# Four small matmul tiles with the complex sum left to the accumulator, in a four-layer FFT kernel on one core

## The chip, the core and the metric

The kernel runs on 1 core of one Trainium2 chip. The metric is the device time of one execution in microseconds. The kernel before has a median of 785.24 us over 3 runs (784.71 to 789.31). One further execution was profiled: it took 786.58 us, and its trace spans 784.8 us, so 1.8 us lie outside the trace. TensorE is called PE (its weight loads PEld), VectorE DVE, ScalarE ACT, GpSimd POOL, SyncE SP.

## The reference

Four residual layers on x (2048 rows, 512 channels), A, B, A, B, each behind a layer norm. All is float32. The weights of both A layers, and of both B layers, are the same.

```python
def _A_ref(x, w_r, w_i):
    X = rfft2(x, axes=(-2, -1)) * (w_r + 1j * w_i)
    return irfft2(X, s=(S, D), axes=(-2, -1))

def _B_ref(u, log_A_real, A_imag, C_real, C_imag, log_dt, D_skip):
    ...
    P = exp((A * dt[:, None])[:, :, None] * pos)       # 512 channels x 128 states x 2048 steps
    K = 2.0 * einsum("dn,dnl->dl", C, P).real
    Kf, Uf = rfft(K, 2 * L), rfft(u_t, 2 * L)          # along time
    return irfft(Uf * Kf, 2 * L)[:, :, :L] + u * D_skip

x = x + _A_ref(layernorm(x), A_w_r, A_w_i)
x = x + _B_ref(layernorm(x), ...)
x = x + _A_ref(layernorm(x), A_w_r, A_w_i)
x = x + _B_ref(layernorm(x), ...)
```

What the change touches is B: a long convolution along time, done as a Fourier transform, a product of complex spectra and a transform back.

## The kernel before

**Stages.** The first A layer fills 0 to about 230 us. From about 120 to 454 us `kernel_time` builds the filter K in 64 half units; on the way its work is spread between that of other stages (the list `FILL`). `kernel_freq` transforms K (four blocks of 128 channels, called K blocks here) and `layer_b` runs the first B layer over four channel blocks b0 to b3, up to about 540 us. Then come the second A layer (to about 668 us) and the second B layer (to the end). In the first B layer the chain of blocks is b0, K1, b1, K2, b2, K3, b3; `kernel_time` steps lie between those of the first part.

**A block of the convolution.** For each block of 128 channels the following steps run; `blk` is the block, and each small matmul goes through the helper `side_by_side`, so that in the profile all of them have line L319 and must be told apart by their tiles.

- `rows` of `forward_b`: the first transform, 64 matmuls of 64x64 weights (a piece of the data, tile `w` or `x`) with 128 columns of the table `t`; then two ACT copies (L651) per four rows into a tile `z`.
- `turn`: eight 32x32-wise transposes on DVE (L657), `z` to `z`.
- `pair`: the second transform, in four pairs i. For each pair and each of two planes (real, imaginary: `pl`) two matmuls with 128x64 weights (table `mb`, half of which is zero, since two groups of 32 channels share it) write one PSUM tile of 128x512.
- `weigh`: the complex product. Per pair, DVE makes the four real products `wb` (L963: two planes of the signal by two planes `kk` of the filter) and a small correction (L965). Four additions or subtractions of 64x512 (L975) then join them into the tile `Y` (`u`): the list `YB` gives 12 of a block's 16 to POOL and 4 to DVE, and `YC`, for the last block of the second layer, 9 and 7.
- `units` of `back`: the first transform back, 8 units of 16 matmuls with weights from `Y`, 128x64, and 64 columns of `mb`; a 32-column matmul (L983) ahead of units 0 and 4; an ACT copy (L988) per unit into `V`. Units 0 to 3 (j=0) need pairs 0 and 1 alone, units 4 to 7 need pairs 2 and 3.
- `rows` of `back`: the second transform back, four times 8 matmuls with 128x64 weights and 128 columns, a DVE addition of 128x512 to the residual (L1002), in the first layer the layer norm's sums (L1007).

In a K block `keep` stands for `weigh`: ACT copies the spectrum into `kk` (L926), from where the first B layer takes it, and SP stores it to DRAM. DVE sets aside the entry at frequency 0 (L934 to L936). The second layer loads the spectra again (`kk<-kf`).

**Order.** `layer_b` writes the order of steps by hand, with those of the block before and the block after between the four pairs of a block:

```python
steps = [[now[0], *turns, *last[:2]], [now[1], *last[2:4], *then[1][:1], *last[4:6]],
         [now[2], *last[6:], *then[1][1:2], *units[:2]], [now[3], *units[2:4], *then[1][2:], *then[2][:4]]]
turns, last = then[2][4:], [*units[4:], *rows]
```

(`now`: pairs with `weigh`; `last`: the rest of the block before; `then[1]`, `then[2]`: `rows` and `turn` of the next block.) A scheduler moves instructions on each engine from there by its own estimate. Buffers are given out in turn: `p1`, `p2` and `p3` are PSUM tiles, with 5 banks for p1 and p3 together and 3 for p2 in the B layers (`PB`). `u` has two buffers (Y and V), `wb` eight, `kk` eight, `kw` (the rounded phases of `kernel_time`) two, `qp` five.

## Time and profile before

| | |
|---|---|
| median of 3 runs | 785.24 us |
| the profiled execution | 786.58 us |
| span of its trace | 784.8 us |
| busy, share of the span: PE, DVE | 612.4 us (78%), 646.6 us (82%) |
| ACT, POOL | 420.4 us (54%), 415.4 us (53%) |
| mean granted TensorE clock | 0.90 |
| DMA | 80.26 MB, mean 102 GB/s |

Busy time is the time in which at least one instruction of an engine was running; several small matmuls that run side by side count once. The `mean ns` of a group is that of one instruction. A float32 matmul of the code stands as two instructions in the trace: the 1024 matmuls of `units` in both layers are 2048 rows. Shares over the whole span mix stages with different limits, so the stages are read one by one.

### The profile page before, as it was taken

What the parts mean: (1) busy time and instruction counts of PE and PEld (TensorE: products, weight loads), DVE (VectorE), ACT (ScalarE), POOL (GpSimd) and SP (SyncE); (2) the same over time, 40 slices, a digit from 0 to 9 for tenths busy, and PEclk for the clock granted to TensorE, in tenths of its full rate; (3) what the DMA queues carried; (4) which work ended last, traced back from release to release, by engine and by line L of the source; (5) the groups of instructions that cost most, each with busy time, mean ns of one, the idle gap of its engine ahead of it and who ended that gap; (6) DMA issues with size and microseconds to landing.
All of it is one profiled execution on the core that took longest, in us unless ns stands there. A gap on an engine that the chain in (4) does not pass through costs nothing. (4 is left out here: it accounts for less than half of the span.)

```text
span 784.8 us, 20886 instructions
## 1 busy us (share of the span) xinstructions
PE 612.4 (78%) x8208; PEld 417.6 (53%) x8208; DVE 646.6 (82%) x1301; ACT 420.4 (54%) x919; POOL 415.4 (53%) x596
## 2 busy tenths in 40 slices
PE   3337788698758687897867977865899897889986
PEld 2336566464424342654343645644877664466666
DVE  7999749889997769968996977878587598789993
ACT  3434788755556676787477833323766335243322
POOL 3675886766625226732675166281055473375850
PEclk9656999998975999899989999997999898799998
DMA  8300651343547232452326359422122004134403
GB/s 320 117 0 1 147 124 49 102 101 129 125 161 148 72 105 49 129 139 79 43 67 146 113 120 252 133 82 81 54 82 83 28 14 147 56 91 128 145 24 105
DMA packets 144257, 80.26 MB, mean 102 GB/s; under 512 B 78656, under 2 KB 123840, under 8 KB 143264
## 3 DMA queue, kind: packets, MB, share of 16 engines
q1 hardware_dynamic: 143904, 78.51, 36.0%
q8 instruction: 65, 1.06, 0.5%
q0 software_dynamic: 256, 0.43, 0.3%
q14 instruction: 32, 0.26, 0.1%
HBM read 54.30 MB, written 25.03 MB: 101 GB/s over the span
## 5 line engine op out<-in xcount | busy, mean ns | idle before, releaser
L975 POOL TENSOR_TENSOR u<-wb,wb 64x512 f32<-64x512 f32 x90 | 137.0, 1523 | 81.2 <-DVE wb L963 74.5
L319 PE MATMUL p<-z,mb 128*64 128x512 f32 (+1 forms) x480 | 104.0, 543 | 13.2 <-DVE wb L963 5.8
L651 ACT COPY z<-p 128x512 f32<-128x512 f32 x96 | 51.5, 595 | 70.5 <-PE p L319 47.0
L861 DVE TENSOR_TENSOR qp<-qp,mag 128x1024 f32<-128x1024 f32 x64 | 83.3, 1305 | 1.2
L963 DVE TENSOR_TENSOR wb<-p,kk 128x512 f32<-128x512 f32 x128 | 80.6, 674 | 4.0 <-PE p L319 4.0
L859 DVE SCALAR_TENSOR_TENSOR qp<-qp,mag 128x256 f32<-128x256 f32 x128 | 63.6, 512 | 18.7 <-ACT qp L805 18.4
L319 PEld LDWEIGHTS p<-mb,u 128*64 128x64 f32 x2048 | 67.6, 146 | 17.9 <-issue 9.6
L319 PE MATMUL p<-mb,u 128*64 128x64 f32 x2048 | 69.9, 231 | 8.6 <-DVE u L975 4.2
L657 DVE STREAM_TRANSPOSE z<-z 128x512 f32<-128x512 f32 x96 | 58.5, 673 | 21.1 <-ACT z L651 21.1
L1087 POOL TENSOR_SCALAR w<-w,norms 128x128 f32<-128x128 f32 x64 | 37.8, 604 | 62.7 <-DMA w<-h 59.7
L530 DVE TENSOR_TENSOR w<-wt,p 128x514 f32<-128x514 f32 x64 | 42.5, 687 | 32.4 <-PE p L319 24.2
L535 POOL TENSOR_TENSOR w<-w,w 64x257 f32<-64x257 f32 x48 | 40.0, 834 | 53.7 <-DVE w L530 45.8
L872 PEld LDWEIGHTS pv<-qp 128*32 128x32 f32 x2048 | 38.0, 120 | 53.8 <-issue 20.2
L805 ACT ACTIVATE kf<-pk 128x512 f32<-128x512 f32 x64 | 38.8, 606 | 48.7 <-PE pk L841 48.4
L459 PE MATMUL p<-w,w 128*128 128x128 f32 x128 | 32.1, 429 | 40.6 <-DVE w L452 30.9
L319 PEld LDWEIGHTS p<-z,mb 128*64 128x64 f32 x480 | 34.4, 142 | 50.5 <-issue 30.9
L319 PE MATMUL p<-t,w 64*64 64x128 f32 x1024 | 48.1, 309 | 16.7 <-DMA w<-kt 8.1
L872 PE MATMUL pv<-qp 128*32 128x64 f32 x2048 | 51.6, 240 | 8.2 <-DVE qp L861 5.3
L988 ACT COPY u<-p 128x512 f32<-128x512 f32 x64 | 37.4, 589 | 38.1 <-PE p L319 38.1
L840 DVE TENSOR_SCALAR kw<-pk 128x512 bf16<-128x512 f32 x64 | 43.0, 679 | 13.3 <-PE pk L839 13.3
L319 PEld LDWEIGHTS p<-t,w 64*64 64x64 f32 x1024 | 36.8, 152 | 29.0 <-DMA w<-kt 10.7
L459 PEld LDWEIGHTS p<-w,w 128*128 128x128 f32 x128 | 27.8, 318 | 44.6 <-issue 24.7
(198 smaller groups left out, 1498.1 us busy)
## 6 DMA issues: line engine op xcount, KB each, us to landing
wt<-in_w SPq DMA_DIRECT2D x32, 257.0 KB
kf<-kk SPq DMA_DIRECT2D x32, 256.0 KB
kk<-kf SPq DMA_DIRECT2D x32, 256.0 KB
u<-in_x SPq DMA_DIRECT2D x16, 256.0 KB
hr<-in_x SPq DMA_DIRECT2D x16, 256.0 KB
kt<-stage SPq DMA_DIRECT2D x32, 128.0 KB
h<-hr SPq DMA_DIRECT2D x16, 256.0 KB
w<-kt SPq DMA_DIRECT2D x32, 128.0 KB
```

The costliest lines, as they stand in the source:

```text
L319: last = self.nc.tensor.matmul(out, weights, data, start=not more, stop=True, skip_group_check=True).ins
L459: nc.tensor.matmul(p[:, b], xf[:, b], t, start=True, stop=True)
L530: nc.vector.tensor_mul(m[pl], W, px[:, None, :].to_broadcast([128, 2, 257]))
L535: e[0].tensor_sub(Y[0:64, v], m[0][hs, 0], m[1][hs, 1])
L651: nc.scalar.copy(tiles["z"][:, :, :, b, m:m + 2].rearrange("p u j m r -> p (u j) (m r)"), ps[b].rearrange("p u j m r -> p (u j) (m r)"))
L657: nc.vector.transpose(tiles["zt"][:, u:u + 8].rearrange("p u j d -> p (u j d)"), tiles["z"][:, u:u + 8].rearrange("p u j b m r -> p (u j b ...
L840: nc.vector.tensor_scalar(whole, p, MAGIC, -MAGIC, op0=ALU.add, op1=ALU.add)
L859: nc.vector.scalar_tensor_tensor(QP[:, c, 0], QP[:, c, 1, :, ::-1], -1.0 if c else 1.0, m[:, 0], op0=ALU.mult, op1=ALU.mult)
L861: nc.vector.tensor_mul(t, t, mag[:, None, 1:3, 256 * j:256 * j + 256].to_broadcast([128, 2, 2, 256]))
L872: nc.tensor.matmul(p[32 * t:32 * t + 32, g], QP[:, c, 2, d], QP[:, c, 0:2, d], start=c == 0, stop=c == 1, tile_position=(0, 32 * t), skip_ ...
L963: nc.vector.tensor_mul(split(m[c, pl], "du", [32, 16]), by_channel(p), split(k[c], "du", [32, 16]))
L975: self.added = e[0].tensor_sub(y[0:64], v[0, 0], v[1, 1]), e[1].tensor_add(y[64:128], v[0, 1], v[1, 0])
```

## The change

**Quarter tiles.** `rows` of `forward_b` now uses weights of 64x32 (twice as many matmuls, eight positions instead of four). `pair` uses 64x64 weights: the contraction is over 64 rows, so the zeros of the old table are gone, and a PSUM tile of 128x512 is made by two matmuls in each of two tiles q at once. `pair` takes a list of tables `kinds`.

**The complex sum in PSUM.** In the first layer `pair` uses the table `DUP`, which makes the real and the imaginary plane of the signal's spectrum in two copies of its rows ("signal products doubled"); DVE multiplies each by the filter's spectrum as it lies in `kk`. In the second layer `pair` uses the plain table `NAT`, and each plane of the filter is loaded from DRAM with its rows doubled ("second K loaded doubled"). Either way there are 16 products of 128x512 per block as before, but they go to two tiles M[0] and M[1], and no addition joins them. `units` multiplies M[0] and M[1] by two tables and lets PSUM add: 64 matmuls of 64x64 per unit of eight channels, 4 units per block. `rows` of `back` does likewise with 64x64 weights, and adds to the residual in halves of 256 columns (L1035 of the new kernel). A step `mix` of four 32-column matmuls replaces the two L983.

**Order and buffers.** Every unit contracts over all four pairs, so units come after `now[3]`, with the next block's `turn` between them. `u` has three buffers (M[0], M[1], V). The buffers of `wb` and `xw` are gone, `w` serves the residual too and has six buffers instead of seven, `kw` one instead of two, `qp` four instead of five, and `kernel_time` ends a half unit three steps after it begins it instead of four (`LAGV`). PSUM has 4 and 4 banks in the B layers (`PB`). The spectra are stored from ACT's queue, and the output from POOL's for the first three blocks (`DQ`). The second A layer's `even` lies in `kk`.

The core of the diff:

```diff
-DQ = ''
+DQ = 'UaOg'
-PB = [5, 3]
+PB = [4, 4]
-LAGV = 4
+LAGV = 3
-QP = 5
+QP = 4
...
-        def pair(i, use):
-            last = None
-            for pl in range(2):
-                p = self.ps("p2", [512])
-                products = []
-                for h in (1, 0):
...
-                    products += [(o[:, 0], MB[:, 0, pl], z[:, 0])] * c + [(o[:, c:], MB[:, 1, pl], z[:, u + c:u + 16])]
-                last = self.side_by_side(products, last)
-                use(pl, p)
+        def pair(i, use, kinds):
+            z = tiles["zt"]
+            last = None
+            for x, K in enumerate(kinds):
+                ps = [self.ps("p2", [512]) for q in range(2)]
+                products = []
+                for first in (1, 0) if i == 0 else (0,):
+                    us = slice(16 * i, 16 * i + 1) if first else slice(16 * i + (i == 0), 16 * i + 16)
+                    for j in range(2):
+                        for q in range(2):
...
+                            products.append((o, K[64 * q:64 * q + 64, 1 - first], z[64 * q:64 * q + 64, us, j]))
+                last = self.side_by_side(products, last)
+                for q in range(2):
+                    use(x, q, ps[q])
...
-            def use(pl, p):
-                for c in range(2):
-                    m[c, pl] = self.sb("wb", [512])
-                    nc.vector.tensor_mul(split(m[c, pl], "du", [32, 16]), by_channel(p), split(k[c], "du", [32, 16]))
...
-                self.added = e[0].tensor_sub(y[0:64], v[0, 0], v[1, 1]), e[1].tensor_add(y[64:128], v[0, 1], v[1, 0])
+            own = kept is not None
...
+                        part = bass.AP(tensor=part.tensor, offset=part.offset, ap=[part.ap[0], [0, 2], part.ap[1]])
+                        self.dma("W")(k[x][q], part)
+                        if i == 0:
+                            nc.gpsimd.tensor_copy(split(k[x][q], "du", [32, 16])[:, :, 0], self.kf0[:, blk, q, x])
+            def use(x, q, p):
+                for o in (x,) if own else range(2):
+                    nc.vector.tensor_mul(M[o][:, q, :, 16 * i:16 * i + 16], by_channel(p),
+                                         split(k[q] if own else k[o][q], "du", [32, 16]))
+            pairs[i](use, self.DUP if own else self.NAT)
...
-                p = self.ps("p3", [64, 8])
-                self.side_by_side([(p[64 * r:64 * r + 64, :, i], Y[:, j, d + i], MBT[:, 64 * r:64 * r + 64])
-                                   for i in range(8) for r in range(2)])
+                ps = [self.ps("p3", [64, 8]) for j in range(2)]
+                self.side_by_side([(ps[j][64 * q:64 * q + 64, :, i], m[64 * j:64 * j + 64, q, d + i],
+                                    self.MT[64 * j:64 * j + 64, x], *[True] * x)
+                                   for i in range(8) for x, m in enumerate(M) for j in range(2) for q in range(2)])
...
+            steps = [now[0], *last[:1], *special, now[1], *last[1:], now[2], *then[1][:2], now[3], *then[1][2:]]
+            turns = then[2]
+            for n in range(4):
+                steps += [*units[n:n + 1], *turns[2 * n:2 * n + 2]]
+            last = rows
```

Three places show what moves. In the second B layer, DVE at the start of the last block has this order before (L963 a product, L965 the correction, L975 an addition of two products into Y, which is `u`):

```order
L963 TENSOR_TENSOR wb_8560<-p_1709_8556,kk_8552 128x512
L963 TENSOR_TENSOR wb_8562<-p_1709_8556,kk_8553 128x512
L963 TENSOR_TENSOR wb_8568<-p_1712_8564,kk_8552 128x512
L965 TENSOR_TENSOR wb_8568<-p_1712_8564,kf_1_65 64x32
L963 TENSOR_TENSOR wb_8571<-p_1712_8564,kk_8553 128x512
L963 TENSOR_TENSOR wb_8627<-p_1720_8624,kk_8620 128x512
L963 TENSOR_TENSOR wb_8629<-p_1720_8624,kk_8621 128x512
L975 TENSOR_TENSOR u_7827<-wb_8560,wb_8571 64x32x16
```

and now this (L993 a product, into one of the two M tiles; L1035 the residual of the block before):

```order
L993 TENSOR_TENSOR u_9289<-p_1734_11386,kk_11378 128x32x16
L993 TENSOR_TENSOR u_9290<-p_1734_11386,kk_11380 128x32x16
L993 TENSOR_TENSOR u_9289<-p_1735_11387,kk_11379 128x32x16
L993 TENSOR_TENSOR u_9290<-p_1735_11387,kk_11381 128x32x16
L1035 TENSOR_TENSOR za_6500<-za_6500,p_1727_11299 128x4x2x32 x2
L1035 TENSOR_TENSOR za_6500<-za_6500,p_1728_11300 128x4x2x32 x2
L993 TENSOR_TENSOR u_9289<-p_1742_11476,kk_11468 128x32x16
```

The additions of products are gone, and the residual's additions stand between the products. On PE, where a block of the second layer gives way to the next, the last four units stand directly ahead of the next block's first pair before:

```order
L319 MATMUL p_1690_8413<-mb_2788,u_7827 64x64 x16
L319 MATMUL p_1691_8431<-mb_2788,u_7827 64x64 x16
L319 MATMUL p_1700_8471<-mb_2788,u_7827 64x64 x16
L319 MATMUL p_1701_8489<-mb_2788,u_7827 64x64 x16
L319 MATMUL p_1709_8556<-z_8547,mb_2788 64x512
```

Now all 256 matmuls of the block's units (64 to a unit) stand behind the next block's `rows`; this is where they begin, four positions in turn, first M[0], then M[1] onto the same columns:

```order
L330 MATMUL p_1617_9643<-t_8859,x_8863 32x64x2
L330 MATMUL p_1618_9678<-mb_2805,u_9289 64x64 x2
L330 MATMUL p_1619_9679<-mb_2805,u_9289 64x64 x2
L330 MATMUL p_1618_9678<-mb_2805,u_9290 64x64 x2
L330 MATMUL p_1619_9679<-mb_2805,u_9290 64x64 x2
```

On DVE at the end of `kernel_time` (L861 before, L888 now, is its last multiplication), the sums of b1 and the transposes of b2 follow it before, ahead of b2's products:

```order
L861 TENSOR_TENSOR qp_5203<-qp_5203,mag_4831 128x2x512
L1007 BN_STATS stats_66<-xw_5465 128x6 x4
L1007 BN_STATS stats_66<-xw_5500 128x6 x4
L657 STREAM_TRANSPOSE z_5598<-z_5378 128x512 x8
L963 TENSOR_TENSOR wb_5644<-p_1116_5640,kk_5234 128x512
```

Now b2's products follow it at once, since those sums and transposes have moved in front of it:

```order
L888 TENSOR_TENSOR qp_5886<-qp_5886,mag_5437 128x2x512
L886 SCALAR_TENSOR_TENSOR qp_5987<-qp_5987,mag_5437 128x256 x2
L888 TENSOR_TENSOR qp_5987<-qp_5987,mag_5437 128x2x512
L993 TENSOR_TENSOR u_3391<-p_1104_6503,kk_6014 128x32x16
L993 TENSOR_TENSOR u_3391<-p_1105_6504,kk_6015 128x32x16
```

More of the change, by code (lines that the diff above doesn't have):

```diff
@@ L1025, in layer_b @@
                     f()
-            now, units, rows = pairs, [], []
+            now, units, rows, special = pairs, [], [], []
             if blk is not None:
-                now = [partial(weigh, blk, pairs, i, *[YC] * (not more and blk == 3)) for i in range(4)]
+                now = [partial(weigh, blk, pairs, i) for i in range(4)]
                 units, rows = back(blk)
+                special = [mix]
             then = chain[i + 1] if i + 1 < len(chain) else (None, [], [])
@@ L1034, in layer_b @@
                 then = chain[-1]
-            steps = [[now[0], *turns, *last[:2]], [now[1], *last[2:4], *then[1][:1], *last[4:6]],
-                     [now[2], *last[6:], *then[1][1:2], *units[:2]], [now[3], *units[2:4], *then[1][2:], *then[2][:4]]]
-            turns, last = then[2][4:], [*units[4:], *rows]
-            steps = sum(steps, [])
+            steps = [now[0], *last[:1], *special, now[1], *last[1:], now[2], *then[1][:2], now[3], *then[1][2:]]
[3 more added lines that the diff above has]
+            last = rows
             half = len(steps) // 2
@@ L1155, in net_kernel @@
             at = cuts[1]
-            wide, folds, banks = ExitStack(), ExitStack(), ExitStack()
+            wide, folds, banks, second = ExitStack(), ExitStack(), ExitStack(), ExitStack()
             def switch():
@@ L1191, in net_kernel @@
         interleave(A[2])
+        second.close()
+        banks.close()
+        outer.enter_context(net.phase("pd", P, p1=(2048, PB[0]), p2=(2048, PB[1]), p3="p1"))
+        outer.enter_context(net.phase("kk", side="right", kk=(2048, 8)))
         net.layer_b(kf, T, out.rearrange("(p n) d -> p n d", n=16), x=h)
```

251 lines of the change are left out of this document (136 added, 115 removed).

## Prediction

> **What bounds the kernel now.** The page's first two lines come first, since they say which engines can be a limit at all.
>
> ```profile
> span 784.8 us, 20886 instructions
> PE 612.4 (78%) x8208; PEld 417.6 (53%) x8208; DVE 646.6 (82%) x1301; ACT 420.4 (54%) x919; POOL 415.4 (53%) x596
> ```
>
> DVE and PE are each busy for about four fifths, so neither bounds the whole, and I split the span where a B layer's limits change. The second row's stage ends at the first residual addition of b3, the third runs from the first product of the second B layer to the end. Columns: window, length, busy us and instructions of PE, PEld, DVE, ACT, POOL, then granted clock, DMA share, GB/s.
>
> ```profile
> 290.00:454.00 164.00, 134.75 (x2343) 77.27 (x2344) 146.08 (x244) 113.84 (x222) 85.72 (x84) 0.91 0.39 95
> 454.00:533.00 79.00, 59.62 (x1086) 43.75 (x1079) 58.57 (x105) 26.60 (x52) 47.24 (x50) 0.96 0.54 146
> 677.00:785.00 108.00, 93.51 (x1800) 69.35 (x1796) 88.97 (x132) 32.87 (x64) 62.35 (x45) 0.97 0.34 100
> 724.00:749.00 25.00, 23.54 (x462) 17.01 (x460) 23.46 (x35) 9.46 (x19) 16.59 (x12) 1.00 0.44 129
> ```
>
> Up to 454 us DVE is 89% busy: it bounds. From 454 to 533 nobody is above 75%: a chain of steps bounds. In a middle block of the second layer (724 to 749) both PE and DVE are at 94%: a block costs 25 us, and only less work on **both** makes it shorter. The timeline gives the marks: where `kernel_time` ends, b3's first sum in the first layer, the first products of blocks of the second layer, and its last two sums (start, length, idle time before it).
>
> ```profile
> 452.74 1.22 DVE L861 TENSOR_TENSOR qp<-qp,mag 128x1024 f32<-128x1024 f32 x1
> 533.38 0.69 DVE L1002 TENSOR_TENSOR za<-xw,p 128x512 f32<-128x512 f32 x1 [7.52 <-PE p L319]
> 677.00 1.25 DVE L963 TENSOR_TENSOR wb<-p,kk 128x512 f32<-128x512 f32 x2
> 723.86 1.89 DVE L963 TENSOR_TENSOR wb<-p,kk 128x512 f32<-128x512 f32 x3 [0.80 <-PE p L319]
> 748.86 1.89 DVE L963 TENSOR_TENSOR wb<-p,kk 128x512 f32<-128x512 f32 x3 [0.16 <-PE p L319]
> 777.84 0.69 DVE L1002 TENSOR_TENSOR za<-za,p 128x512 f32<-128x512 f32 x1 [8.75 <-PE p L319]
> 780.46 0.69 DVE L1002 TENSOR_TENSOR za<-za,p 128x512 f32<-128x512 f32 x1 [0.19 <-PE p L319]
> ```
>
> Both ends of a B layer, 533.38 and 777.84, show DVE waiting 7.5 and 8.8 us for PE: after the last products there is only the chain of additions, units and rows.
>
> **DVE and POOL, part by part.** These are the groups removed (busy total, then mean ns of one), and of the corrections one row each by line (min, median, max ns).
>
> ```profile
> L975 POOL TENSOR_TENSOR u<-wb,wb 64x512 f32<-64x512 f32 x90 | 137.0, 1523 | 81.2 <-DVE wb L963 74.5 <-DVE wb L965 1.4
> L975 DVE TENSOR_TENSOR u<-wb,wb 64x512 f32<-64x512 f32 x38 | 46.4, 1221 | 0.5
> L965 DVE TENSOR_TENSOR wb<-p,kf x16: 189/203/205, 294.8 to 758.9; 64x32 f32<-64x32 f32 x16
> L934 DVE TENSOR_SCALAR kf<-kk,kc x8: 229/235/965, 273.9 to 510.6; 64x32 f32<-64x32 f32 x8
> L963 DVE TENSOR_TENSOR wb<-p,kk 128x512 f32<-128x512 f32 x128 | 80.6, 674 | 4.0 <-PE p L319 4.0
> L585 DVE TENSOR_TENSOR w<-p,w 128x256 f32<-128x256 f32 x32 | 13.2, 413 | 8.1 <-ACT w L582 7.9
> ```
>
> POOL loses 137 us and DVE 46.4; also 16 corrections of 0.20 (3.2) and three times eight small ones of about 0.24 (5.9; L935 and L936 have L934's shape). The 128 products stay, at a start-to-start of 0.63 us (three in 1.89). The 32 residual additions of 0.69 become 64 of 256 columns; L585 is that shape, 0.41: 26.4 instead of 21.5, so +4.9. DVE's sum is -50.6. On its path I count 38 x 1.22 where they stood: 19 in the second B layer (-23), 11 between 454 and 533 (-13), 8 before 454 (-10).
>
> **PE.** The columns of the work stay, the pieces get smaller, and all hangs on how many run at once. The timeline groups instructions that start side by side:
>
> ```profile
> 416.31 0.65 PE L872 MATMUL pv<-qp 128*32 128x64 f32 x32
> 459.59 1.98 PE L319 MATMUL p<-t,w 64*64 64x128 f32 x64 [0.72 <-issue]
> 718.95 3.25 PE L319 MATMUL p<-mb,u 128*64 128x64 f32 x104
> L319 PE MATMUL p<-mb,u 128*64 128x64 f32 x2048 | 69.9, 231 | 8.6 <-DVE u L975 4.2 <-POOL u L975 2.1 <-issue 1.5
> L319 PE MATMUL p<-t,w 64*64 64x128 f32 x1024 | 48.1, 309 | 16.7 <-DMA w<-kt 8.1 <-issue 5.7 <-POOL w L1087 2.1
> L872 PE MATMUL pv<-qp 128*32 128x64 f32 x2048 | 51.6, 240 | 8.2 <-DVE qp L861 5.3
> L319 PE MATMUL p<-z,mb 128*64 128x512 f32 (+1 forms) x480 | 104.0, 543 | 13.2 <-DVE wb L963 5.8
> ```
>
> A row of the timeline lasts from its first start to its last end, so start to start is its length, less the mean length of one from the groups beside it, over the count less one. Weights of 128x64 leave two positions: (3.25 - 0.23) / 103 = 29.3 ns a piece. Four positions of 64x64 with 128 columns: (1.98 - 0.31) / 63 = 26.5. Four positions 32 wide with 64 columns: (0.65 - 0.24) / 31 = 13.2. Halving the columns or doubling the positions halves the time per piece, so four quarter tiles with 64 columns should come at 13.2 to 14.7 ns; I take **14.5**. Then:
> - units: 2048 rows x 29.3 = 60 us become 4096 x 14.5 = 59. Even.
> - rows of `back`: 512 rows of 128 columns become 2048 of 64 at a quarter of the time each or so (two positions to four, half the columns). Even.
> - rows of `forward_b`: twice the rows, eight positions instead of four: 1536 x 26.5 = 41 us stay 41 if eight positions run at once. No row shows eight; if only four do, it is 81, +40 in all, some +10 in the second layer. I take the even value, as the rows with two and four positions both scale, and keep the other for the range.
> - `pair`: 104 us for 12 blocks, 8.7 a block. Without the zeros a K block and a block of the second layer need half the passes; a block of the first layer makes two copies and stays. 8 x 4.3 = -35 us, half of it in the second layer.
>
> [...]
>
> **The second B layer.** Two more durations are needed, the transposes of a block and the copy of a unit.
>
> ```profile
> 460.01 4.87 DVE L657 STREAM_TRANSPOSE z<-z 128x512 f32<-128x512 f32 x8 [4.50 <-ACT z L651]
> L988 ACT COPY u<-p 128x512 f32<-128x512 f32 x64 | 37.4, 589 | 38.1 <-PE p L319 38.1
> ```
>
> Units now need all four pairs, so the block becomes two phases in turn. Products: 16 x 0.63 + 8 residual halves x 0.41 = 13.4 us of DVE. Then the turn-over on PE: 512 unit instructions x 14.5 ns = 7.4, the next block's first pair 1.1 (a quarter of 4.3), some 1 for its start: 9.5, during which DVE has only transposes (4.9). Block 0 takes 10.1 + 9.5 = 19.6, blocks 1 and 2 22.9 each against 25.0 (748.86 - 723.86), the last 13.4, then units 7.4, copy 0.6, rows 3.8 (256 x 14.7 ns), two additions 0.8 and what follows the last addition now, 784.8 - 781.15 = 3.65: together 30. Sum 95.4, against 784.8 - 677.0 = 107.8: -12. I take **-8**, as the sum has no small waits; -12 and 0 are its ends.
>
> **The first B layer and K.** Up to 454 us DVE bounds. It loses 10 + 3 (eight L975 and half the small corrections) and gains 6, since eight transposes (4.9) and four sums (1.1) now stand ahead of the end of `kernel_time`. New waits: `kw` has one buffer, so DVE's next phase (queue behind it: `qp`, products) waits for PE's reading of the last.
>
> ```profile
> L840 DVE TENSOR_SCALAR kw<-pk 128x512 bf16<-128x512 f32 x64 | 43.0, 679 | 13.3 <-PE pk L839 13.3
> L841 PE MATMUL pk<-kw,ni 128*128 128x512 bf16 x64 | 25.1, 409 | 5.4 <-DVE kw L840 5.4
> L1007 DVE BATCH_NORM_STATS2 stats<-xw 128x6 f32<-128x128 f32 x32 | 7.1, 278 | 0.0
> ```
>
> That costs between 0 and 64 x 0.41 = 26 us. Other work mostly stands between two phases in DVE's order, so with `qp` four and a lag of three I take 3, near the lower end. `kernel_time` ends at about 451 instead of 454. From there the chain is b2's products (0.5 + 10.1), its units with K3's transposes beneath (7.4), K3's pairs (4.3 + 0.5), b3's transposes (4.9), b2's sums (8 x 0.41 + 16 x 0.22 = 6.8), b3's products (10.1), units and copy (8.1), half its rows (1.9): 54.6, against 533.38 - 453.96 = 79.4. That is -25, with the 3 before it -28; I take **-20** for waits left out, with -28 and +6 (the 26 of `kw` against the 20) as ends. The second A layer between is untouched but for where `even` lies.
>
> **Transfers.** The page gives the loads of the second layer and the traffic in 40 slices.
>
> ```profile
> kk<-kf SPq DMA_DIRECT2D x32, 256.0 KB
> GB/s 320 117 0 1 147 124 49 102 101 129 125 161 148 72 105 49 129 139 79 43 67 146 113 120 252 133 82 81 54 82 83 28 14 147 56 91 128 145 24 105
> ```
>
> The doubled loads make 32 x 256 KB into 64, so 16.8 MB in some 100 us, besides 4.2 MB of output: 210 GB/s. A slice has moved 320 and 252, and between 724 and 749 a share of 0.44 moved 129, so 293 at full share. I take no cost; 8.4 MB more at 293 would be 29 us if none of it were hidden, the upper end. The stores of the spectra go from SP's to ACT's queue; ACT, 54% busy, has room for 32 issues.
>
> Sum: 786.6 - 20 - 8 = 758.6 for an execution like the profiled one, which stands 1.3 above the median, so 757 to 758. **Predicted: 758.**
>
> **Rivals.**
> - *Slower: quarter tiles do not overlap fourfold.* If 64-column pieces stay at 29 ns, the turn-over of every block grows by 512 x 14.8 = 7.6 for its units and 256 x 14.7 = 3.8 for its rows, 11.4 in all, and nothing lies beside it, since the next products wait for the units to have read M. The second layer has four, +45; of the first layer's four the two behind 454 us count in full, +23, the others as far as DVE has no other work, 0 to 23. On 758.6 that is 827 to 850, and 815 if PE's present idle time takes up some 10. It decides from about 19 ns a piece: 68 to 91 us for 14.8 ns more, so the 28 are gone at 4.5 to 6 more. For it: no row shows four 64x64 tiles with 64 columns. Against: `pv` at 13.2. Chance 0.11.
> - *No net gain: the phases alternate.* Each turn-over takes 13.5 instead of 9.5 us, since units, copies, rows and the next pair wait for each other in PSUM's four banks; with seven turn-overs that is 28, the whole gain: 776 to 792, and to 800 with some of `kw`'s 26 on top. For it: DVE has only 4.9 us of work in these 9.5, and the waits of 7.5 and 8.75 us above are such ends. Against: `pair` leaves PE 4.3 less to do per block. Chance 0.17, of which 0.04 above 793.
> - *Supply:* products wait for the doubled loads, as `kk` holds only two pairs ahead. Up to 29 us, half of which falls in the 28 gained: 765 to 795. For it: the slices of that layer, the last six, move 145 at most now. Against: 320 GB/s was reached. Chance 0.06.
> - *Better than thought:* all small waits vanish, both sums as worked out (-12, -28): below 742. Chance 0.04.
>
> The main case, 742 to 775, gets 0.62. The range 740 to 792 leaves out the first rival, the second's tail and some 0.03 below. One per cent, about what a measurement of this kernel can tell from no change, is 777.4 to 793.1. Faster: main, the better case and 0.01 of supply, 0.67. Within: 0.13 of the second rival and 0.04 of supply, 0.17. Slower: 0.11, 0.04 and 0.01, 0.16.
>
> **What will show it.** The new profile should have 4096 unit rows of 64*64 at 14 to 15 ns start to start; `p<-z,mb` near 70 us; no POOL additions; the first product of the second layer to the end in 96 to 100 us; b3's first sum near 510 to 513. Wrong would be: units at 25 ns or more; DVE waiting on DMA in L993; or DVE waiting before L867 (`kw`) for over 10 us in all, by which `kernel_time` would not end before 454.

## The result and the profile after

The changed kernel took **883.32 us** (median of 4 runs, 876.97 to 886.33) against 786.52 us of the kernel before (4 runs, 784.71 to 789.31): a ratio of 1.1217, with a 95% interval of 1.1137 to 1.1296. Predicted were 758 us and a gain of 28; it is a loss of 97. The profiled execution took 880.66 us. The page of its profile begins:

```profile
span 878.9 us, 31603 instructions
PE 640.6 (73%) x13600; PEld 430.5 (49%) x13600; DVE 584.5 (67%) x1255; ACT 417.9 (48%) x919; POOL 282.3 (32%) x542
```

DVE and POOL lost the work that was to go (62 and 133 us, where 50.6 and 137 were worked out), and every engine is now busy for a smaller share of the span, though PE and PEld are busy for longer in us. PE and PEld have 13600 instructions each instead of 8208. The same three stages as before, by windows:

```profile
290.00:504.00 214.00, 158.03 (x4114) 88.63 (x4104) 141.26 (x253) 126.95 (x252) 48.66 (x82) 0.86 0.33 81
504.00:594.00 90.00, 66.74 (x2188) 44.74 (x2192) 35.85 (x73) 22.73 (x47) 10.35 (x10) 0.92 0.42 112
737.00:879.00 142.00, 97.21 (x4008) 78.21 (x4008) 64.52 (x120) 30.90 (x60) 12.82 (x28) 0.88 0.42 137
```

In the second B layer (last row) DVE is busy for 64.5 of 142 us, and nobody above 69%. The marks are the same instructions as in the prediction: the last multiplication of `kernel_time`, b3's first residual addition, and the first products of the second layer's four blocks.

```profile
502.93 1.23 DVE L888 TENSOR_TENSOR qp<-qp,mag 128x1024 f32<-128x1024 f32 x1
594.43 1.42 DVE L1035 TENSOR_TENSOR za<-w,p 128x256 f32<-128x256 f32 x4 [17.11 <-PE p L330]
736.74 4.84 DVE L993 TENSOR_TENSOR u<-p,kk 128x512 f32<-128x512 f32 x8
764.29 4.87 DVE L993 TENSOR_TENSOR u<-p,kk 128x512 f32<-128x512 f32 x8 [9.52 <-issue]
800.87 4.88 DVE L993 TENSOR_TENSOR u<-p,kk 128x512 f32<-128x512 f32 x8 [8.04 <-issue]
839.21 4.88 DVE L993 TENSOR_TENSOR u<-p,kk 128x512 f32<-128x512 f32 x8 [8.86 <-issue]
```

| us | `kernel_time` ends | from there to b3's first sum | to the second layer's first product | from there to the end |
|---|---|---|---|---|
| before | 454.0 | 79.4 | 143.6 | 107.8 |
| worked out | 451 | 54.6, taken as 62 | as before | 95.4, taken as 100 |
| after | 504.2 | 90.3 | 142.3 | 142.1 |
| difference to before | +50.2 | +10.9 | -1.3 | +34.3 |

The last three marks are 36.6 and 38.3 us apart, where 22.9 was worked out. What fills such a block is seen in PE's timeline (start, length, count, idle time before), first the rows of `forward_b`, then the units:

```profile
776.60 2.73 PE L330 MATMUL p<-t,x 64*32 64x128 f32 x127 [2.94 <-issue]
783.58 3.23 PE L330 MATMUL p<-t,x 64*32 64x128 f32 x107 [4.25 <-issue]
786.74 3.52 PE L330 MATMUL p<-mb,u 64*64 64x64 f32 x148
791.11 2.10 PE L330 MATMUL p<-mb,u 64*64 64x64 f32 x128 [0.85 <-issue]
794.58 2.09 PE L330 MATMUL p<-mb,u 64*64 64x64 f32 x128 [1.38 <-issue]
798.05 1.79 PE L330 MATMUL p<-mb,u 64*64 64x64 f32 x107 [1.38 <-issue]
```

Within a row the pace is what was predicted: (2.09 - 0.23) / 127 = 14.6 ns a piece, four quarter tiles at once. But after every 128 pieces PE stops for 1.38 us "issue", that is, with nothing in the profile that it waits for. 128 pieces are 256 instructions with their weight loads, and such a stretch comes every 3.47 us (794.58 - 791.11, 798.05 - 794.58): **27.1 ns a piece**. In the second layer the units and the two kinds of rows wait 17.1, 10.4 and 5.7 us for "issue", 33.2 in all, where the layer lost 34.3:

```profile
L330 PE MATMUL p<-mb,u 64*64 64x64 f32 x2048 | 38.7, 237 | 20.6 <-issue 17.1 <-DVE u L993 3.6
L330 PE MATMUL p<-t,x 64*32 64x128 f32 x768 | 17.9, 317 | 10.7 <-issue 10.4
L330 PE MATMUL p<-u,t 64*64 64x64 f32 x1024 | 20.4, 223 | 7.0 <-issue 5.7 <-ACT u L1016 1.2
```

The profile's list of DMA queues shows what comes in that rhythm, before (first row) and after (packets, MB, share):

```profile
q8 instruction: 65, 1.06, 0.5%
```

```profile
q8 instruction: 107, 1.75, 0.8%
```

1.06 MB in 65 packets is 16 KB each; 42 more packets stand against 5392 more matmuls and as many loads, 257 instructions a packet. Between 786 and 800 us nothing else is transferred, so that the traffic in 40 slices of 0.35 us shows the packets alone:

```profile
GB/s 0 0 0 0 0 0 0 47 0 0 0 0 0 0 0 0 0 47 0 0 0 0 0 0 0 0 0 47 0 0 0 0 0 0 0 0 0 0 47 0
```

In the trace they start at 788.51, 792.24, 795.74 and 799.58, and the stretches of units start 2.60, 2.34 and 2.31 us after the first three (791.11, 794.58, 798.05). I read this as PE getting its program in packets of 256 instructions (13600 matmuls and as many loads over 107 packets are 254 each), called pages of instructions from here on: where a page is used up in 2.09 us, PE waits for the next one. In the trace of after no two of these packets start less than 3.33 us apart, and in the second layer 31 of them start in 142 us; 31 x 3.47 = 108 us. Before it was 14 in 108.

Of the runs below, the profiled executions of `wide_units` and `lean` were slower ones of their kernels (spans of 837.8 and 796.3 us), so that their marks stand some 10 us late; medians are over all executions, while the ratios leave such slower ones out.

### The profile page after: what moved, and what is told of

It is laid out like the page before. It is cut to its first block, busy times and chain, and to the rows that moved or that the text cites. A ratio compares the mean times of both kernels' runs of the same rounds, so it can differ in the third digit from the quotient of the medians.

```text
span 878.9 us, 31603 instructions
## 1 busy us (share of the span) xinstructions
PE 640.6 (73%) x13600; PEld 430.5 (49%) x13600; DVE 584.5 (67%) x1255; ACT 417.9 (48%) x919; POOL 282.3 (32%) x542
## 5 line engine op out<-in xcount | busy, mean ns | idle before, releaser
L993 DVE TENSOR_TENSOR u<-p,kk 128x512 f32<-128x512 f32 x128 | 80.5, 683 | 52.7 <-issue 26.4
L330 PE MATMUL p<-mb,u 64*64 64x64 f32 x4096 | 79.3, 233 | 39.7 <-issue 35.4
L330 PE MATMUL p<-z,mb 64*64 64x512 f32 (+2 forms) x704 | 100.2, 551 | 10.0 <-DVE u L993 4.2
L330 PEld LDWEIGHTS p<-mb,u 64*64 64x64 f32 x4096 | 72.9, 147 | 48.1 <-issue 43.5
L888 DVE TENSOR_TENSOR qp<-qp,mag 128x1024 f32<-128x1024 f32 x64 | 78.9, 1234 | 1.9
L330 PE MATMUL p<-t,w 64*32 64x128 f32 x2048 | 53.7, 306 | 21.1 <-DMA w<-kt 10.9
L886 DVE SCALAR_TENSOR_TENSOR qp<-qp,mag 128x256 f32<-128x256 f32 x128 | 54.8, 446 | 20.9 <-ACT qp L832 20.1
L867 DVE TENSOR_SCALAR kw<-pk 128x512 bf16<-128x512 f32 x64 | 43.7, 683 | 27.0 <-PE pk L866 17.0
L330 PEld LDWEIGHTS p<-t,w 64*32 64x32 f32 x2048 | 37.7, 116 | 42.8 <-issue 22.7
L1124 POOL TENSOR_SCALAR w<-w,norms 128x128 f32<-128x128 f32 x64 | 33.0, 534 | 76.9 <-DMA w<-h 39.6
L330 PE MATMUL p<-u,t 64*64 64x64 f32 x2048 | 41.3, 227 | 16.3 <-issue 13.1
L330 PEld LDWEIGHTS p<-z,mb 64*64 64x64 f32 x704 | 27.9, 146 | 48.0 <-issue 17.6
L470 PEld LDWEIGHTS p<-w,w 128*128 128x128 f32 x128 | 27.8, 319 | 44.3 <-issue 24.7
```

Source lines behind the costliest of these rows:

```text
L330: last = self.nc.tensor.matmul(out, weights, data, start=not more, stop=True, skip_group_check=True).ins
L470: nc.tensor.matmul(p[:, b], xf[:, b], t, start=True, stop=True)
L867: nc.vector.tensor_scalar(whole, p, MAGIC, -MAGIC, op0=ALU.add, op1=ALU.add)
L886: nc.vector.scalar_tensor_tensor(QP[:, c, 0], QP[:, c, 1, :, ::-1], -1.0 if c else 1.0, m[:, 0], op0=ALU.mult, op1=ALU.mult)
L888: nc.vector.tensor_mul(t, t, mag[:, None, 1:3, 256 * j:256 * j + 256].to_broadcast([128, 2, 2, 256]))
L993: nc.vector.tensor_mul(M[o][:, q, :, 16 * i:16 * i + 16], by_channel(p), split(k[q] if own else k[o][q], "du", [32, 16]))
```

## The experiments

All times are medians; a ratio is to the kernel before, run on the same chip beside it (its medians there were 786.87 to 793.57). Theory "supply" says that PE waits for its pages of instructions. Its rivals change with the run.

**Bare sequences.** `pages` holds nothing but matmuls, of the shapes in question:

```python
SEQUENCES = (("quarter", 64, 64, 64, 4, 0), ("narrow", 64, 64, 32, 4, 0), ("double", 64, 64, 128, 4, 0),
             ("single", 64, 64, 64, 1, 0), ("loaded", 64, 64, 64, 4, 48), ("eighth", 64, 32, 128, 8, 0),
             ("phase", 128, 32, 64, 4, 0), ("half", 128, 64, 64, 2, 0), ("thin", 64, 64, 16, 4, 0))
```

> Nine bare sequences of 512 matmuls (1024 rows of the trace, 8 pages of 256 instructions with their weight loads) and nothing else of the kernel; the output is not the reference's. ACT's copies lie between them. Positions in turn, columns: quarter (64x64 weights, four positions, 64 columns), narrow (32 columns), thin (16), double (128), single (one position, 64), half (128x64, two, 64), phase (128x32, four, 64), eighth (64x32, eight, 128), loaded (as quarter, with 48 loads of 256 KB beside it). Supply: quarter, narrow, thin and phase all settle at 27 ns a row (3.47 us per 128), in bursts of 128 with a pause, however few the columns; double and half lie just at or above it (27 to 30) with no or short pauses, single near 55 without pause; loaded like quarter or somewhat slower. Eighth: 13 ns inside a burst if eight positions run at once, and 27 on the whole. Rival 'pace' (the pause belongs to this kernel's waits): quarter 14.6, narrow and thin 7 to 13, phase 13 to 15 throughout.

Rows from the timeline of the sequences, two of `quarter`, one of `narrow`, then `loaded`, `eighth`, `half` and `thin`:

```profile
27.49 3.38 PE L38 MATMUL quarter<-a,wts 64*64 64x64 f32 x128 [2.73 <-issue]
33.41 2.63 PE L38 MATMUL quarter<-a,wts 64*64 64x64 f32 x128 [2.54 <-issue]
...
53.83 9.61 PE L38 MATMUL narrow<-a,wts 64*64 64x32 f32 x350 [8.46 <-ACT wts L50]
...
262.89 2.09 PE L38 MATMUL loaded<-a,wts 64*64 64x64 f32 x128 [1.36 <-issue]
266.62 2.09 PE L38 MATMUL loaded<-a,wts 64*64 64x64 f32 x128 [1.64 <-issue]
...
283.14 7.30 PE L38 MATMUL eighth<-a,wts 64*32 64x128 f32 x348 [8.81 <-ACT wts L50]
291.88 2.02 PE L38 MATMUL eighth<-a,wts 64*32 64x128 f32 x128 [1.44 <-issue]
...
348.37 31.63 PE L38 MATMUL half<-a,wts 128*64 128x64 f32 x1024 [1.35 <-ACT a L49]
381.35 27.29 PE L38 MATMUL thin<-a,wts 64*64 64x16 f32 x1024 [1.35 <-ACT a L49]
```

Nothing of the kernel is there, and in `loaded` the pause is: 128 pieces in 2.09 us, then 1.36 to 1.91 us of nothing, a stretch every 3.5 to 4.0 us. `eighth` and `phase` do the same. So the pause belongs to the stream of instructions and not to a wait of the kernel. Nor is it the granted clock, which fell in the second layer from 0.97 to 0.88: from 745 to 782 us of the changed kernel, where the units pause for 1.83 us and three times for 1.38, it was 1.00, and over `eighth` (283 to 311 us), which pauses six times, 0.92. What the lower clock cost besides, no run separates. `half`, the shape of the old units, needs 30.7 ns a piece and never pauses: its page lasts 3.9 us (128 x 30.7 ns), longer than the 3.47 us from page to page in the changed kernel. Two more things follow. The first stretch of `eighth` has 348 pieces without a pause, after 8.8 us in which PE waited. These are 2.7 pages in 7.30 us, in which at 3.47 us a page 2.1 can have come; so the rest lay ready, and a burst of 32 says nothing of the supply. And the loads meant for `loaded` ran early, beside `quarter`, as the windows of the two show, with that of `thin` below (granted clock, DMA share, GB/s at the end):

```profile
6.00:46.00 40.00, 23.98 (x1024) 22.71 (x1024) 0.81 (x3) 0.00 (x0) 0.77 0.93 333
246.00:275.00 29.00, 18.44 (x1024) 17.34 (x1024) 0.40 (x2) 0.00 (x0) 0.93 0.02 4
381.00:409.00 28.00, 27.02 (x1024) 26.70 (x1024) 0.56 (x2) 0.00 (x0) 0.53 0.02 4
```

`thin` had none of the pauses that supply expected, and `narrow` none in its last 418 pieces; both missed the rival's 7 to 13 ns too, `thin` with 26.4 ns a piece. The granted clock accounts for it. This is the last row split where the clock changes (the engines are PE, PEld and ACT):

```profile
381.35:382.85 1.50, 1.50 (x104) 1.50 (x104) 0.00 (x0) 1.00 0.00 0
382.90:409.00 26.10, 25.47 (x932) 25.14 (x924) 0.26 (x1) 0.50 0.02 4
```

At 1.00 a piece of 16 columns takes 14.4 ns (1.50 / 104), where one of 64 takes 14.6. At 0.50 it takes 27.3, and the first 350 pieces of `narrow`, which waited for nothing, took 26.7 ((9.61 - 0.29) / 349), so that a page lasts 3.4 to 3.5 us, as long as the 3.47 us from page to page, and nothing is left to wait for. `single` missed its 55 ns with 107, at a clock of 0.50 as well.

With 333 GB/s of loads beside it a page of `quarter` took up to 5.9 us (33.41 - 27.49), at a clock of 0.77 on the mean. The clock alone does not make that, since a page of `thin` takes 3.5 us at 0.50; the loads are what else differs.

**Fewer instructions, the same columns.** `wide_units` exchanges weights and data in the new units:

```diff
-                self.side_by_side([(ps[j][64 * q:64 * q + 64, :, i], m[64 * j:64 * j + 64, q, d + i],
-                                    self.MT[64 * j:64 * j + 64, x], *[True] * x)
-                                   for i in range(8) for x, m in enumerate(M) for j in range(2) for q in range(2)])
+                self.side_by_side([(ps[j][64 * q:64 * q + 64], self.MT[64 * j:64 * j + 64, x],
+                                    m[64 * j:64 * j + 64, q, d:d + 8], *[True] * x)
+                                   for x, m in enumerate(M) for j in range(2) for q in range(2)])
```

> The changed kernel, but each unit of the transform back swaps weights and data: the table is loaded as weights and 512 columns of M run through it, so that one matmul takes the place of eight (4096 unit rows become 512; the columns that run through the array stay the same; the output of this step comes out transposed, so the values are not the reference's). Theory 'supply' (PE gets its instructions in pages of 256, one page per 3.47 us at best, and 128 small matmuls with their 128 weight loads use one up in 2.09): 28 pages go, each turn-over of a block loses 4 x 1.38 us and more, so the second B layer falls from 142 us by about 25 to 30, the two blocks behind kernel_time by about 13, the two ahead of it by 0 to 13: 825 to 845. Rival 'phases' (units wait for all four pairs and the next products for the units; the number of instructions is not the matter): the columns and the order stay, so within 1% of the changed kernel, 875 to 892.

832.12 us, 1.0495 (1.0383 to 1.0607): inside what supply said, and 51 us below the changed kernel. Packets of instructions fell from 107 to 79, the second layer from 142.1 to 119.7 (by 22, where 25 to 30 were expected), the stage behind `kernel_time` from 90.3 to 74.2. The two blocks inside `kernel_time` gave little, 501.3 against 504.2 for its end. The pace changed a little too, as this row of two units shows, 32 pieces of 512 columns:

```profile
761.04 3.66 PE L330 MATMUL p<-u,mb 64*64 64x512 f32 x32
```

(3.66 - 0.66) / 31 = 97 ns for what eight pieces of 14.6 did, 117: about 10 us of PE in the whole kernel, a fifth of the gain at most.

`lean` also takes the first transform back to 64x64 weights, and the second transform back to 128x64 weights without its sum over r; of its diff, this last part:

```diff
-                self.summed = self.side_by_side([(ps[q][64 * b:64 * b + 64, i], TBT[64 * q:64 * q + 64, r, b, n0 + i],
-                                                  V[64 * q:64 * q + 64, 32 * r + 16 * b + n0 + i].rearrange("p j d -> p (j d)"),
-                                                  *[True] * r)
-                                                 for i in range(8) for r in range(2) for q in range(2) for b in range(2)])
+                self.summed = self.side_by_side([(ps[r][64 * b:64 * b + 64, i], TBT[:, r, b, n0 + i],
+                                                  V[:, 32 * r + 16 * b + n0 + i].rearrange("p j d -> p (j d)"))
+                                                 for i in range(8) for r in range(2) for b in range(2)])
```

> As wide_units, and further the first transform with 64x64 weights again (half the rows) and the second transform back with 128x64 weights (half the rows, not summing over r; values are not the reference's): pages fall from 107 to about 59, columns and order stay. Supply: the second B layer 103 to 108 us, from kernel_time's end to b3's first sum 60 to 68, kernel_time to end near 476 (what the buffers cost alone): 785 to 805. Phases: what is left over 95 in the second layer after wide_units comes from the order of units and products, so at most 10 below wide_units: 815 to 832.

789.74 us, 0.9972 (0.9925 to 1.0019): the whole loss of 12% is gone with 48 of the 107 packets, and the phases were not the matter. That it lies in the expected 785 to 805 is luck in part: the second layer came out shorter than the 103 to 108 expected, and the end of `kernel_time` later than 476. Its blocks of the second layer begin 19.0, 21.6 and 22.6 us apart, where 19.6, 22.9 and 22.9 were worked out, and the layer took 93.3 us:

```profile
703.02 4.84 DVE L987 TENSOR_TENSOR u<-p,kk 128x512 f32<-128x512 f32 x8
722.03 4.88 DVE L987 TENSOR_TENSOR u<-p,kk 128x512 f32<-128x512 f32 x8 [1.72 <-issue]
743.63 4.88 DVE L987 TENSOR_TENSOR u<-p,kk 128x512 f32<-128x512 f32 x8 [1.41 <-issue]
766.22 4.88 DVE L987 TENSOR_TENSOR u<-p,kk 128x512 f32<-128x512 f32 x8 [1.04 <-issue]
```

But the gain of 28 did not come either, since `kernel_time` still ended at 493.1 instead of 454. The window from b0's first product to that end, and the list of waits in it (total us, times, longest), show DVE busy for 146 of 209 us and waiting at the blocks' products and sums for PE, with `kernel_time`'s steps in line behind:

```profile
284.00:493.00 209.00, 162.04 (x2460) 79.41 (x2459) 145.64 (x259) 128.70 (x255) 51.45 (x82) 0.80 0.33 82
```

```profile
DVE u L987 <- PE p L330: 18.8, 8, 7.7
DVE w L1028 <- PE p L330: 18.6, 4, 9.7
DVE qp L880 <- ACT qp L826: 16.0, 23, 3.0
```

**Why `kernel_time` ends late.** Three runs have the kernel before with parts of the change that add no instruction: the buffers (`before_buffers`), the order of steps (`late_units`), and both. First the buffers (of the last line only what changes):

```diff
-LAGV = 4
+LAGV = 3
-QP = 5
+QP = 4
-kw=(1024, 2)
+kw=(1024, 1)
```

> The kernel before with the new kernel's buffers of kernel_time alone: kw one instead of two, qp four instead of five, the half unit ended three steps behind instead of four. Rival 'buffers' (the 50 us that kernel_time ends later come from these): 810 to 836. Supply: kernel_time there is bound by DVE, its waits for PE come from the units and rows of the blocks between, so at most +10: 783 to 796.

The core of the change of order:

```diff
-            steps = [[now[0], *turns, *last[:2]], [now[1], *last[2:4], *then[1][:1], *last[4:6]],
-                     [now[2], *last[6:], *then[1][1:2], *units[:2]], [now[3], *units[2:4], *then[1][2:], *then[2][:4]]]
-            turns, last = then[2][4:], [*units[4:], *rows]
+            steps = [now[0], *last[:2], now[1], *last[2:], now[2], *then[1][:2], now[3], *then[1][2:]]
+            turns = then[2]
+            for n in range(8):
+                steps += [*units[n:n + 1], *turns[n:n + 1]]
+            last = rows
```

> The kernel before with the new kernel's order of steps alone: all eight units of a block stand behind its last pair, with the next block's transposes between them, and the rows beside the next block's pairs; tiles, tables, additions and buffers as before, so the instructions and pages are those of before. lean, with hardly more instructions than before, still ended kernel_time late (493 us in its profile against 454), with DVE idle for 63 of the 209 us from b0's first product against 18 of 164. Theory 'order' (DVE's and PE's queues put products, sums and units in blocks ahead of kernel_time's steps, and these wait in line): kernel_time ends at 470 to 490; in the second layer units no longer lie beside products, 7.5 us a block less what PE had to wait anyway, 110 to 130; 810 to 845 in all. Rival 'buffers' (kw, qp and the lag made that delay): kernel_time ends within 6 of 454, and only the second layer is longer.

> As late_units, with kw one, qp four and the lag of three. If order and buffers add up (22 us was the buffers' part of kernel_time's end in before_buffers): kernel_time ends some 20 later than in late_units, 490 to 510. If both are the same thing, a pipeline that is emptied once: within 8 of late_units.

| | median, ratio (95%) | `kernel_time` ends | to b3's first sum | second layer |
|---|---|---|---|---|
| before | | 454.0 | 79.4 | 107.8 |
| `before_buffers` | 804.49, 1.0182 (1.0103 to 1.0261) | 476.0 | 75.0 | 107.7 |
| `late_units` | 804.67, 1.0190 (1.0109 to 1.0272) | 474.5 | 80.5 | 106.1 |
| `late_units_buffers` | 816.02, 1.0337 (1.0279 to 1.0395) | 488.2 | 77.8 | 108.3 |
| `lean` | 789.74, 0.9972 (0.9925 to 1.0019) | 493.1 | 68.5 | 93.3 |
| after | 883.32, 1.1217 (1.1137 to 1.1296) | 504.2 | 90.3 | 142.1 |

Buffers alone cost 22 us of that end, the order alone 20, both 34, less than the sum: so in the kernel before these two make most of the 50 us without pages or tiles, and some 16 are left to supply and the rest, which no run splits. `before_buffers` lies between its two expected ranges, `late_units` below its own, since only its end of `kernel_time` came as expected. The profile of before is from another chip, where it took 785 us, so single marks compare to a few us only; by the ratios the three cost 14, 15 and 27 us in all. In the second layer the order alone costs nothing (106.1), where I had expected 110 to 130: it took as long with all units behind the products as with half of them between.

`lean_old_buffers` gives `lean` the old `kw`, `qp` and lag (M[0] and M[1] then share a tile).

> As lean, with kw two, qp five and the lag of four as in the kernel before, for which M[0] and M[1] share one tile (order and sizes as before). Supply with buffers: kernel_time ends some 20 us earlier, near 455, everything behind it as in lean: 762 to 785. If the buffers matter only together with a PE that is short of instructions: as lean, within 8 us.

804.21 us, 1.0177 (1.0076 to 1.0277): no gain but a loss of 14 to `lean`, `kernel_time`'s end at 496.7. So the buffers no longer decide in `lean`, though in `late_units_buffers` they cost 14 us on top of the order, or the shared tile costs what they bring; this run can't tell the two apart. More buffers for the kernel before bring next to nothing (the second run also has LAGV = 5):

```diff
-QP = 5
+QP = 6
-kw=(1024, 2)
+kw=(1024, 3)
```

> The kernel before with kw three and qp six instead of two and five: the other direction of before_buffers, which lost 22 us at kernel_time's end. DVE is idle for 18 of the 164 us there, 9.4 of them before kw for PE, so at most 18 can be gained: if waits for a free buffer made these idle times, 770 to 783; if two and five are enough, within 1% of before, 781 to 797.

> As kw3_qp6, and the half unit ended five steps behind instead of four. If the depth of the pipeline is what fewer buffers took away, 768 to 783; if it is deep enough, 781 to 797; a longer lag also ends each group of units later, so up to 800 is possible.

791.15 us, 0.9987 (0.9942 to 1.0031), and 785.76 us, 0.9965 (0.9933 to 0.9997): two, five and four were nearly enough, and one less of each was not. The second is the fastest version that was run, 0.35% below the kernel before, at the edge of what its interval tells from no change.

**Instructions added to the kernel before.** `before_halves` splits each unit matmul in two.

```diff
-                self.side_by_side([(p[64 * r:64 * r + 64, :, i], Y[:, j, d + i], MBT[:, 64 * r:64 * r + 64])
-                                   for i in range(8) for r in range(2)])
+                self.side_by_side([(p[64 * r:64 * r + 64, 32 * c:32 * c + 32, i], Y[:, j, d + i], MBT[:, 64 * r + 32 * c:64 * r + 32 * c + 32])
+                                   for i in range(8) for c in range(2) for r in range(2)])
```

> The kernel before, but each unit matmul with 64 columns of the table is made as two with 32 columns: 2048 unit rows become 4096, the columns and everything else stay. Supply: 16 pages more, a block's units take 512 x 27.1 ns = 13.9 us instead of 7.5, so +6.4 for each of the four blocks of the second layer, where PE is 94% busy, and for the two blocks behind kernel_time, 0 to 13 for the two others: 820 to 838. Phases: nothing is changed in the order, 780 to 794.

856.58 us, 1.0841 (1.0751 to 1.0931), more than supply had said; the second layer took 137.5 us, `kernel_time` ended at 485.1. But the timeline shows no pause in these units:

```profile
784.89 7.66 PE L319 MATMUL p<-mb,u 128*64 128x32 f32 x256
```

That is 29 ns a piece, as with 64 columns: half the columns made a piece no shorter. So this run shows that small pieces have a price by number, but not that pages are it; it was badly chosen for that, and the agreement in the second layer is chance.

`before_pair32` tries what might have beaten both: the old kernel with the zeros of `pair` taken out by 64x32 weights. The core of its diff, without the first transform:

```diff
-                    o = p[64 * h:64 * h + 64].rearrange("p (u d) -> p u d", d=32)
-                    products += [(o[:, 0], MB[:, 0, pl], z[:, 0])] * c + [(o[:, c:], MB[:, 1, pl], z[:, u + c:u + 16])]
+                        for q in range(2):
+                            o = p[64 * h + 32 * q:64 * h + 32 * q + 32].rearrange("p (u d) -> p u d", d=32)
+                            z = tiles["zt"][64 * q:64 * q + 64, :, i // 2]
+                            products.append((o[:, us.start - u:us.stop - u], MB[64 * q:64 * q + 64, 1 - first, pl], z[:, us]))
```

> The kernel before with one idea of the change alone, in another form: the second transform uses the zeros' place, as four 64x32 weights side by side instead of two 128x64 with half zeros, and the first transform 64x32 weights so that the rows lie as that needs; products, additions and units as before. PE's pair time should halve (104 to 52 us), 12 pages are added among 65. Supply: no stage comes near a page per 3.47 us, so nothing is lost, and the second layer, where PE and DVE are both at 94%, gains 0 to 6 us as DVE stays: 776 to 788. Phases expects the same.

815.66 us, 1.0316 (1.0231 to 1.0401), slower where both theories expected no loss. `before_rows32` has only its first transform:

> The kernel before with the first transform alone in 64x32 weights, eight positions, as the new kernel and before_pair32 have it (1536 rows become 3072; the halves of the channels come out in another order, so the values are not the reference's); the second transform stays as before. before_pair32 was 25 us slower although its second transform has half the passes. Supply: 256 rows of a block take 2 pages, 6.9 us instead of 3.4, in twelve blocks, of which those behind kernel_time and in the second layer show: this kernel is as slow as before_pair32 or slower, 812 to 830. If the second transform in 64x32 is what costs, this one stays within 1% of before, 781 to 797.

793.99 us, 1.0105 (1.0016 to 1.0194): both expectations missed. In its second layer the rows lie between other work and wait 0.5 us for "issue", where those of the changed kernel wait 10.4. This fits a supply that counts over all that PE runs in a stretch, and not over the small pieces alone, as I had counted. The rows account for a third, all of it up to the end of `kernel_time` (464.3, in `before_pair32` 465.3); the other two thirds come with the second transform in 64x32 pieces, 9 us between there and b3's first sum and 8 in the second layer, where the products of `before_pair32` wait 10.2 us for PE (3.7 in the kernel before). Why, stays open.

## Where the prediction went wrong

- **The step that failed is "units: 2048 rows x 29.3 = 60 us become 4096 x 14.5 = 59. Even."** The pace was right, 14.6 ns with four tiles at once, and so the first rival in its own terms (tiles don't overlap fourfold) was wrong. But the pace holds for one page of 256 instructions. Over pages a piece costs 27.1 ns: 111 us for the units instead of 59, and a block's 512 take 13.9 instead of 7.4. The row that settled four tiles, 32 pieces in 0.65 us, was a quarter of a page, and the longest that the prediction read, 104 pieces, was less than one. The trace of before hardly shows the wait: the 0.72 us of "issue" ahead of the row at 459.59, which I took out of the pace, are no sign of it, since the stretches above that waited started 2.31 to 2.60 us after a packet, and none starts here between 453.30 and 458.88. What it did show was the 65 packets of 16 KB, and the prediction did not count them.
- **"Rows of `back`: even", "rows of `forward_b`: even"** failed in the same way. Eight positions do run at once (in `eighth`, (2.02 - 0.29) / 127 = 13.6 ns), but 256 pieces of each in a block are two pages each, 6.9 us. With the units a block has 1024 small pieces, 8 pages, 27.8 us, against 462 matmul rows in the whole 25 us before, large ones among them. That is more than the 22.9 worked out for the block, and since most of DVE's work does not lie beside them, 36.6 to 38.3 came of it.
- **Layer 2 as worked out** (95.4): near, once the instructions are there; `lean` took 93.3. Since its units take some 6.2 us a block (64 x 97 ns, by the row of `wide_units`) instead of 7.4, about 5 us less in all, some 3 of the 4 us taken off for small waits are there too. And the rival "the phases alternate" was wrong for that layer: neither `lean` nor `late_units` shows it.
- **"Up to 454 us DVE bounds. It loses 10 + 3 ... and gains 6"** failed by assuming that DVE goes on to bound. After the change it is busy for 141 of 214 us there, and its longest waits from 290 to 504 name the steps of the blocks:

```profile
DVE w L1035 <- PE p L330: 30.1, 4, 13.9
DVE qp L886 <- ACT qp L832: 14.6, 17, 5.1
DVE kw L867 <- PE pk L866: 10.4, 4, 5.1
```

- L1035, the residual's addition, waits for PE's rows, and `kernel_time`'s steps stand behind it in DVE's queue: after the wait of 13.9 us the next one (L867) starts at 362.52, behind the sums of 359.64 and 360.97. I had named that queue only for `kw`. In the kernel before the order alone costs 20 us there, and `kw`, `qp` and the lag 22 where they stand alone, 14 on top of the order, for which the prediction took 3 out of 0 to 26: the bound held, the choice near its lower end was wrong.
- **From there to b3's first sum** (54.6, taken as 62): 90.3, and still 68.5 in `lean`. So besides supply some 6 us over what was taken are left; for these the cause stays open.
- **Transfers**: right. The group of the products waited 1.8 us for `kk` in all, and 0.5 in the second layer of `lean`, which took no longer than was worked out:

```profile
L993 DVE TENSOR_TENSOR u<-p,kk 128x512 f32<-128x512 f32 x128 | 80.5, 683 | 52.7 <-issue 26.4 <-PE p L330 24.2 <-DMA kk<-kf 1.8
```

- **Pair, -35 us**: not settled. The group's busy time is 100.2 instead of 104.0 us, but its pieces now lie between others, so that this time no longer measures them; and `before_pair32`, where they are halved in another way, lost.
- The chances: the slower side had 0.16, for another mechanism and with its price (815 to 850) too low, since the loss in `kernel_time` comes on top. Two of the signs named for being wrong came: units over 25 ns, and 10.4 us before L867 up to 504.

## What to carry to other kernels

Before a matmul is cut into smaller ones, count the instructions of the busiest stretch, weight loads included, and multiply by the time that it took to bring them (13.6 ns each here, 3.47 us for 256): a pace read from a short burst is no price for a long one. Idle time marked "issue" in the middle of a row of equal instructions, every 128 matmuls here, is a sign to follow. And where two engines' queues are written in a fixed order, an engine that bounds a stage bounds it only as long as nothing ahead in its own queue waits; so order and buffers are to be priced apart from the arithmetic: each cost some 15 us of the whole here without one instruction more.

## What the hardware showed that I had not expected

- PE's instructions came in packets of 16 KB, never less than 3.33 us apart in the changed kernel, and after PE had waited for 8.8 us in `eighth`, 348 pieces, 2.7 packets' worth, ran in 7.30 us without a pause.
- The stretches of matmuls that had to wait began 2.31 to 2.60 us after such a packet started (791.11, 794.58 and 798.05 after 788.51, 792.24 and 795.74 in the changed kernel).
- A piece of 16 or 32 columns was hardly cheaper than one of 64: 29 ns with 32 columns in two positions (7.66 us for 256) where 64 took 29.3, and in four positions 14.4 ns with 16 columns at a clock of 1.00 where 64 took 14.6; at 0.50 it was 27.3.
- A bare row of matmuls in one position ran at a granted clock of 0.50, and needed 107 ns a piece (109.49 us for 1024); the sequences with two and more positions and 64 columns and more had 0.90 to 0.95 when no loads ran beside them.

```profile
135.00:245.00 110.00, 109.49 (x1024) 109.30 (x1024) 6.61 (x13) 0.00 (x0) 0.50 0.00 1
```
